# Spectral filter and SoLU expert on one core: a later landing of the transposes in the plan that orders the instructions

## The chip, the cores and the metric

The kernel runs on one core of a Trainium2 chip. The metric is the device time of one execution in microseconds, and the number compared is the median over runs.

## The reference

x is (8, 3136, 256). For each of the 8 batches the sequence goes through a real FFT, is multiplied with a complex 256 x 256 matrix, gets a bias, is soft-thresholded at 0.01, and goes back through the inverse FFT. The 25,088 rows that come out then go through a two-matrix layer:

```python
h = x @ w_in                                  # 256 -> 1024
sm = softmax(h);  solu = h * sm
ln = (solu - mean(solu)) / sqrt(var(solu) + 1e-6) * g_ln
out = ln @ w_out                              # 1024 -> 256
```

## The kernel before

**The FFT.** 3136 is split as 98 x 32. Each batch goes through four small products on TensorE (fwd1, fwd2, inv1, inv2, with the complex product, mix, in the middle), with two round trips through DRAM (tiles s1 and s2). Values are carried as pairs of fp16 numbers, a high and a low part. Results of inv2 are written into a ring (ring_hi, ring_lo).

**The layer.** It works on 196 tiles of 128 rows, 24 or 25 in a batch. A tile takes three steps. moe_head multiplies the ring with w_in into two PSUM banks (ph, 12 matmuls), VectorE finds the maximum (nm), ScalarE the exponential and VectorE the product (u). moe_turn splits u into lh (ScalarE) and ll (GpSimd) and issues two DMAs from the SP queue that transpose them: lh into th, ll into tl, 128 x 1024 fp16 each. moe_tail multiplies th with both parts of w_out (16 matmuls) and tl with one (8 matmuls) into a bank po; ScalarE scales po into o, and one to three DMAs on the SP queue store it. There are three buffers each for th and tl, two each for lh and ll, four for u, two for o; of the 8 PSUM banks at most 5 are ph and at most 2 po.

**The order.** No engine's order is written by hand. A class Plan collects all operations with a key (their wished place), gives each a length in ns (weigh, L304), plays them through on a model of the five engines (order, L351), and issues them sorted by the start times of that model (issue, L341). In every step of order, each engine looks at the operations whose inputs are ready; among those that can start within 50 ns of the earliest it takes the one with the smallest key. The engine with the earliest start goes first. After that an operation's end tells when its readers are ready (plus a delay by engine, 90 ns for a DMA) and when its buffers come free. The model's times are used for the order alone: on the chip each engine runs its instructions in that order and waits on semaphores for the real landings. All instructions stand under line L349 in the trace, that of the call, so tiles tell them apart.

**A DMA in the model.** weigh gives it a time on the SP queue (length) and a time on a shared bus (moved): 1600 and 1500 ns for a transpose, 430 ns and bytes/270 for the others. order then does:

```python
op.end = free[e] = at + op.length
...
if op.moved:
    bus = max(bus, op.end) + op.moved
    op.end = bus + 2000.0
```

So in the model a transpose that finds queue and bus free ends 1600 + 1500 + 2000 = 5100 ns after its start.

Of the kernel before, what the change touches and what calls it, by code (L numbers as in the profile page):

```python
# [242 lines left out]
class Plan:  # L243
# [60 lines left out]
    def weigh(self, op, name, args, kw, ins, outs):  # L304
        if name == "dma_start":
            v = next(v for v in (*outs, *ins) if not isinstance(v, DramView))
            size = (v.rows[1] - v.rows[0]) * v.cells.size * mybir.dt.size(v.dtype)
            cross = kw.get("transpose", False)
            op.length += 1600.0 if cross else 430.0
            op.moved += 1500.0 if cross else size / 270.0  # L310
        elif op.engine == "tensor":
            moving = ins[-1]
            n = moving.cells.size * (4 if moving.dtype == F32 else 1) * 0.42 + 1
            name = ins[0].tile.kw["name"]
            op.split = 2 if "gb" in name else 4 if name == "fa16_s" else 1
            op.length += n / op.split
        else:
            big = max((v.cells.size for v in (*ins, *outs)), default=1)
            scalars = sum(v.cells.size == 1 for v in ins)
            if big == 1:  # L320
                scalars -= 2 if name == "tensor_tensor" else 1
            each = self.ELEMENT[op.engine]
            wide = [v for v in ins if v.cells.size > 1]
            sbuf = not any(v.tile.kind.banks for v in (*ins, *outs))
            if op.engine == "scalar" and sbuf:
                each = 0.87
            if op.engine == "gpsimd" and len(wide) == 2 and all(v.dtype == F32 for v in (*wide, *outs)):
                each = 2.12
            if op.engine == "vector" and sbuf and name in ("tensor_scalar", "tensor_copy") and big > 1:
                each, op.port = 0.545, True  # L330
            if op.engine == "vector" and sbuf and len(wide) == 2:
                op.port = True
            if op.engine == "gpsimd":
                op.port = True
            op.length += self.CALL[op.engine] + big * each + max(scalars, 0) * self.SCALAR[op.engine]
            if "accum_out" in kw and op.engine == "scalar":
                op.length += 92.0
            if ALU.pow in kw.values() or ALU.pow in args:
                op.length += 420.0
# [11 lines left out]
    def order(self):  # L351
        ready = {e: [] for e in self.ENGINES}
        free = dict.fromkeys(self.ENGINES, 0.0)
        waits, bus, split, port = {}, 0.0, 1, 0.0
        for op in self.ops:
            waits[op] = len(op.needs)
            for o in op.needs:
                o.next.append(op)
            if not op.needs:
                op.at = 0.0  # L360
                ready[op.engine].append(op)
        left = {t: len(t.users) for op in self.ops for t in op.tiles}

        turn, turns = {}, {}
        for t, op in sorted(((t, min(t.users, key=lambda op: op.seq)) for t in left), key=lambda x: (x[1].key, x[1].seq)):
            if t.kind.banks is None:
                turn[t] = turns.get(t.kind, 0)
                turns[t.kind] = turn[t] + 1
        done = []

        def may_start(op):
            at = max(free[op.engine], op.at, port if op.port else 0.0)
            taken = {}
            for t in op.tiles:
                if t.owner is None:
                    k = t.kind
                    n = len(k.placed) + taken.get(k, 0)
                    taken[k] = taken.get(k, 0) + 1
                    if turn.get(t, n) != n:
                        return np.inf  # L380
                    n -= k.bufs
                    if n >= 0:
                        at = max(at, k.freed[n] if n < len(k.freed) else np.inf)
                    if k.banks is not None:
                        n, spare = taken.get(k.banks, 0), k.banks.free
                        taken[k.banks] = n + 1
                        at = max(at, spare[n][0] if n < len(spare) else np.inf)
            return at

        while len(done) < len(self.ops):  # L390
            best = None
            for e in self.ENGINES:
                can = [(may_start(op), op) for op in ready[e]]
                if not can:
                    continue
                first = min(at for at, _ in can)
                if first == np.inf:
                    continue
                _, _, at, op = min((op.key, op.seq, at, op) for at, op in can if at <= first + self.PATIENCE)
                if best is None or at < best[0]:  # L400
                    best = at, op
            assert best is not None, "the plan is stuck"
            at, op = best
            e = op.engine
            ready[e].remove(op)
            if e == "tensor":
                if op.split != split:
                    at += 100.0 if split == 1 else 220.0
                split = op.split
            op.start = at  # L410
            op.end = free[e] = at + op.length
            if op.port:
                port = op.end
            if op.moved:
                bus = max(bus, op.end) + op.moved
                op.end = bus + 2000.0
            for t in op.tiles:
                if t.owner is None:
                    t.owner = op
                    t.kind.placed.append(t)  # L420
                    if t.kind.banks is not None:
                        t.bank = t.kind.banks.free.pop(0)[1]
                left[t] -= 1
                if not left[t]:
                    freed = max(o.end + self.SEEN[o.engine] for o in t.users)
                    insort(t.kind.freed, freed)
                    if t.kind.banks is not None:
                        insort(t.kind.banks.free, (freed, t.bank))
            for o in op.next:
                waits[o] -= 1  # L430
                if not waits[o]:
                    o.at = max(p.end + (0.0 if p.engine == o.engine == "tensor" else self.SEEN[p.engine]) for p in o.needs)
                    ready[o.engine].append(o)
            done.append(op)
        self.span = max(op.end for op in done)
        return sorted(done, key=lambda op: (op.start, op.seq))
# [830 lines left out]
```

## Time and profile before

| | |
|---|---|
| median of 3 runs | 1628.03 us (1625.98 to 1630.09) |
| the profiled execution | 1626.85 us |
| its span, first to last instruction | 1625.1 us |
| TensorE (PE) matmuls busy | 1564.6 us (96%) |
| VectorE (DVE) busy | 1332.9 us (82%) |
| ScalarE (ACT) busy | 1242.8 us (76%) |
| GpSimd (POOL) busy | 1121.0 us (69%) |
| mean granted TensorE clock | 0.985 |

PE stands for matmuls and PEld for the weight loads that run beside them; the weights of the product with w_out are th and tl, so a late transpose shows first as a wait of PEld and then of PE. SPq is the SP queue, which issues every DMA. A matmul's end is modelled from its own latency, so matmuls that follow each other closely overlap in the records.

### The profile page before, as it was taken

The page shows a single profiled execution, that of the slowest core. Times are in us where ns is not written, and L with a number is a line of the kernel's source. Part 1 is how long each engine was busy: PE and PEld are TensorE (multiplying, and loading weights), DVE is VectorE, ACT ScalarE, POOL GpSimd, SP SyncE. Part 2 cuts the span into 40 slices and gives each one's busy share as a digit, 9 for nine tenths or more (in the row PEclk, how much of TensorE's full clock was granted, in tenths as well). Part 3 has the DMA queues.
Part 4 walks back from the last instruction along what each step waited for, and adds up shares of the span by engine and source line. Part 5 has one row for each costly group of instructions (what it writes and reads, how often), then busy time and mean ns, then how long its engine had stood idle before and what let it go on. Part 6 is the DMA issues. An engine that isn't in the chain of part 4 may idle for free.

```text
span 1625.1 us, 39102 instructions
## 1 busy us (share of the span) xinstructions
PE 1564.6 (96%) x13328; PEld 1107.1 (68%) x13328; DVE 1332.9 (82%) x3423; ACT 1242.8 (76%) x2576; POOL 1121.0 (69%) x1890
## 2 busy tenths in 40 slices
PE   5979999899999999999999999999999999999998
PEld 3645877468765777667766687666776577776675
DVE  4779899988998888887978789788887879877774
ACT  4667777886788867897778877788678877788886
POOL 0555777657875688667876578766876677776775
PEclk8989999999999999999999999999999999999999
DMA  8878987898898975789669995789857994587765
GB/s 235 272 226 209 230 230 173 205 221 216 200 210 169 209 175 127 161 185 213 161 126 171 190 200 132 147 177 205 188 124 148 181 198 124 128 156 146 141 130 110
DMA packets 540649, 290.30 MB, mean 179 GB/s; under 512 B 429660, under 2 KB 505982, under 8 KB 540450
## 3 DMA queue, kind: packets, MB, share of 16 engines
q1 hardware_dynamic: 540450, 287.81, 78.8%
q8 instruction: 104, 1.70, 0.4%
q14 instruction: 95, 0.78, 0.1%
HBM read 107.88 MB, written 77.07 MB: 114 GB/s over the span
## 4 chain that ended last, share of the span: by engine, by line
PE 79%; DMA 7%; DVE 5%; ACT 4%; issue 2%; POOL 1%; SPq 1%; DVEq 0%; ACTq 0%; POOLq 0%
PE po L349 27%; PE ph L349 24%; PE pf L349 23%; PE pb L349 4%; DMA th<-lh 3%; DMA tl<-ll 2%; DVE u L349 1%; ACT u L349 1%; SPq L349 1%; DVE nm L349 1%; POOL ll L349 1%; ACT junk L349 1%; DVE xl L349 1%; ACT lh L349 0%; DMA zt<-s2f 0%
## 5 line engine op out<-in xcount | busy, mean ns | idle before, releaser
L349 POOL TENSOR_TENSOR ll<-u,lh 128x1024 f16<-128x1024 f32 x196 | 420.6, 2146 | 136.5 <-ACT lh L349 111.1
L349 PE MATMUL po<-wout,th 128*128 128x256 f16 x3136 | 379.7, 275 | 18.2 <-DMA th<-lh 18.0
L349 PEld LDWEIGHTS <-th 128*128 128x128 f16 x3136 | 305.1, 99 | 88.7 <-DMA th<-lh 26.3
L349 ACT ACTIVATE u<-ph,m,hsb 128x512 f32<-128x512 f32 x384 | 296.1, 777 | 75.0 <-DVE m L349 74.7
L349 DVE TENSOR_REDUCE nm<-ph 128x1 f32<-128x512 f32 x392 | 265.8, 686 | 91.9 <-PE ph L349 90.5
L349 DVE SCALAR_TENSOR_TENSOR u<-ph,ch,u 128x512 f32<-128x512 f32 x392 | 282.2, 748 | 28.5 <-ACT u L349 12.7
L349 PE MATMUL ph<-win_hi,ring_hi 128*128 128x512 f16 x768 | 291.9, 380 | 1.2 <-DVE u L349 1.2
L349 PE MATMUL ph<-win_low,ring_lo 128*128 128x512 f16 x768 | 291.5, 380 | 0.0
L349 PE MATMUL ph<-win_lo,ring_hi 128*128 128x512 f16 x768 | 291.5, 380 | 0.0
L349 ACT CAST lh<-u 128x1024 f16<-128x1024 f32 x196 | 205.4, 1048 | 78.3 <-DVE u L349 74.4
L349 PEld LDWEIGHTS <-ring_hi 128*128 128x128 f16 x1536 | 145.7, 98 | 137.8 <-issue 10.8
L349 ACT ACTIVATE junk<-u,total 128x1024 bf16<-128x1024 f32 x196 | 226.0, 1153 | 6.4 <-POOL total L349 6.3
L349 PE MATMUL po<-wout,tl 128*128 128x256 f16 x1568 | 203.9, 273 | 9.1 <-DMA tl<-ll 9.1
L349 POOL TENSOR_TENSOR y<-yt,yc 128x512 f32<-128x512 f32 (+1 forms) x104 | 136.6, 1314 | 69.8 <-ACT yt L349 33.1
L349 PEld LDWEIGHTS <-tl 128*128 128x128 f16 x1568 | 150.6, 98 | 42.8 <-DMA tl<-ll 12.7
L349 PE MATMUL pf<-w_hi,Xl 128*128 128x256 f16 (+1 forms) x546 | 148.8, 273 | 1.1 <-DVE Xl L349 1.1
L349 PE MATMUL pf<-w_hi,Xh 128*128 128x256 f16 (+1 forms) x546 | 149.2, 273 | 0.0
L349 PE MATMUL pf<-w_lo,Xh 128*128 128x256 f16 (+1 forms) x546 | 148.8, 273 | 0.0
L349 POOL TENSOR_TENSOR yl<-y,yh 128x512 f16<-128x512 f32 (+1 forms) x104 | 124.0, 1193 | 34.0 <-ACT yh L349 32.3
L349 PEld LDWEIGHTS <-ring_lo 128*128 128x128 f16 x768 | 75.2, 98 | 91.0 <-DVE peaks L349 0.3
L349 ACT ACTIVATE o<-po,r 128x256 f32<-128x256 f32 x196 | 93.4, 476 | 56.2 <-PE po L349 42.6
L349 PEld LDWEIGHTS <-Xh 128*128 128x128 f16 (+1 forms) x1196 | 113.5, 99 | 26.4 <-issue 1.9
(197 smaller groups left out, 2843.1 us busy)
## 6 DMA issues: line engine op xcount, KB each, us to landing
xt<-in_x_dram SPq DMA_DIRECT2D x60, 392.0 KB
zt<-s SPq DMA_DIRECT2D x56, 392.0 KB
s<-zout SPq DMA_DIRECT2D x42, 512.0 KB
xt<-in_x_dram SPq DMA_DIRECT2D x96, 192.0 KB
s<-av SPq DMA_DIRECT2D x96, 192.0 KB
bin<-s SPq DMA_DIRECT2D x36, 512.0 KB
out_dram<-o SPq DMA_DIRECT2D x128, 96.0 KB
out_dram<-o SPq DMA_DIRECT2D x136, 64.0 KB
```

What stands on the lines that cost most here:

```text
L349: getattr(engine, name)(*args, **kw)
```

## The change

A transpose gets a further attribute, late, of 3000 ns (0 for any other DMA), and order adds it to the time at which the model believes that it has ended. The time on the SP queue and on the bus stay as they were. No operation, buffer, size or key changes.

```diff
             cross = kw.get("transpose", False)
             op.length += 1600.0 if cross else 430.0
             op.moved += 1500.0 if cross else size / 270.0
+            op.late = 3000.0 if cross else 0.0
...
             if op.moved:
                 bus = max(bus, op.end) + op.moved
-                op.end = bus + 2000.0
+                op.end = bus + 2000.0 + op.late
```

## Rows read from the trace of the kernel before

**Rows 1.** The page, part 1: busy time, share of the span and instructions of each engine.

```profile
PE 1564.6 (96%) x13328; PEld 1107.1 (68%) x13328; DVE 1332.9 (82%) x3423; ACT 1242.8 (76%) x2576; POOL 1121.0 (69%) x1890
```

**Rows 2.** The page, part 4: the chain that ended last, shares of the span by engine.

```profile
PE 79%; DMA 7%; DVE 5%; ACT 4%; issue 2%; POOL 1%; SPq 1%; DVEq 0%; ACTq 0%; POOLq 0%
```

**Rows 3.** Waits, whole span: who waited for whom, us in total, times, longest us.

```profile
PEld L349 <- DMA th<-lh: 26.3, 23, 4.7
...
PE po L349 <- DMA th<-lh: 18.0, 14, 4.6
...
POOL ll L349 <- DMA tl<-ll: 20.5, 11, 3.9
...
PEld L349 <- DMA tl<-ll: 12.7, 11, 1.8
...
PE po L349 <- DMA tl<-ll: 9.1, 10, 1.5
```

**Rows 4.** Groups of instructions: busy us, mean ns of one, idle before and its releasers.

```profile
L349 POOL TENSOR_TENSOR ll<-u,lh 128x1024 f16<-128x1024 f32 x196 | 420.6, 2146 | 136.5 <-ACT lh L349 111.1 <-DMA tl<-ll 20.5 <-ACT u L349 2.9
...
L349 PE MATMUL ph<-win_hi,ring_hi 128*128 128x512 f16 x768 | 291.9, 380 | 1.2 <-DVE u L349 1.2
```

**Rows 5.** Windows of 50 us: busy time (instructions) by engine, granted clock, DMA share, GB/s.

```profile
50.00:100.00 50.00, 50.00 (x347) 27.39 (x347) 36.76 (x64) 36.32 (x73) 35.47 (x30) 1.00 0.78 247
...
300.00:350.00 50.00, 42.46 (x361) 28.04 (x359) 41.97 (x128) 40.58 (x82) 28.17 (x57) 0.93 0.94 209
...
600.00:650.00 50.00, 50.00 (x472) 36.53 (x472) 41.96 (x109) 37.61 (x84) 42.55 (x64) 1.00 0.57 126
...
1250.00:1300.00 50.00, 46.23 (x366) 29.26 (x365) 44.05 (x117) 44.14 (x88) 30.95 (x64) 0.99 0.90 181
```

**Rows 6.** Timeline around the longest stall: start us, us, engine, work, idle before and releaser.

```profile
315.58 0.57 SPq L349 DMA_DIRECT2D zt<-s  x1
...
321.47 3.60 PE L349 MATMUL po<-wout,th 128*128 128x256 f16 x16 [4.59 <-DMA th<-lh]
...
324.86 2.03 PE L349 MATMUL pf<-ia_s,zt 98*128 98x98 f16 x24
...
328.00 0.39 PE L349 MATMUL ph<-win_hi,ring_hi 128*128 128x512 f16 x1
```

**Rows 7.** Timeline of two more stalls, and of the SP queue ahead of the second.

```profile
913.76 3.53 PE L349 MATMUL po<-wout,th 128*128 128x256 f16 x16 [2.32 <-DMA th<-lh]
...
1289.55 3.88 SPq L349 DMA_DIRECT2D xt<-in_x_dram  x7
...
1294.80 1.28 SPq L349 DMA_TRANSPOSE th<-lh  x1
...
1298.11 2.40 PE L349 MATMUL po<-wout,th 128*128 128x256 f16 x16 [2.59 <-DMA th<-lh]
```

**Rows 8.** Windows around the drops of the clock, and the last stage.

```profile
320.90:331.00 10.10, 9.53 (x64) 6.62 (x65) 4.52 (x20) 5.18 (x12) 4.16 (x7) 0.72 0.87 200
...
913.00:924.90 11.90, 11.14 (x85) 7.33 (x86) 9.62 (x33) 9.45 (x20) 8.09 (x16) 0.86 1.06 207
...
1299.40:1302.80 3.40, 3.40 (x30) 1.36 (x28) 3.01 (x12) 3.40 (x7) 2.18 (x4) 0.50 1.20 136
1425.00:1608.00 183.00, 183.00 (x1431) 127.10 (x1429) 136.45 (x404) 149.76 (x305) 128.98 (x264) 1.00 0.74 139
```

**Rows 9.** The chain in order of time: start us, us, what (a DMA: issue to release).

```profile
1124.77 7.06 DMA tl<-ll
...
1613.27 3.08 DMA th<-lh
```

**Rows 10.** Timeline of the last two waits of PE.

```profile
1613.57 1.05 PE L349 MATMUL po<-wout,tl 128*128 128x256 f16 x8 [0.41 <-DMA tl<-ll]
1616.39 3.21 PE L349 MATMUL po<-wout,th 128*128 128x256 f16 x16 [1.78 <-DMA th<-lh]
```

**Rows 11.** Groups of the stretch 1420 to 1610, columns as in rows 4.

```profile
L349 PE MATMUL po<-wout,th 128*128 128x256 f16 x557 | 66.5, 273 | 0.0
```

## The prediction

> **What bounds the kernel now.** I read the totals first. PE's matmuls are busy for 96% of the span, and no other engine for more than 82% [rows 1]; the chain that ended last runs over PE for 79% and over DMAs for 7% [rows 2]. So PE sets the pace, and what can be won is the time in which PE stands or runs slowly. The waits say where it stands: 18.0 us for th and 9.1 us for tl, 27.1 us in 24 waits [rows 3], of some 60 us that PE idles in all (1625.1 - 1564.6 [rows 1]). Waits of PE for anything computed are nearly absent: the first matmul of ph, the group behind which VectorE's delay would show, lost 1.2 us in 768 [rows 4]. The plan's picture of the engines is thus good, and what it misjudges are these two transposes.
>
> The windows show when. In stretches like 600 to 650 us PE has no gap, at a DMA share of 0.57; in 300:350 and 1250:1300 it lacks 7.5 and 3.8 us, at shares of 0.94 and 0.90 [rows 5]. The timeline shows what a stall costs beyond its gap. The longest took 4.59 us, and the 16 matmuls behind it 3.60 us [rows 6]; the granted clock of 320.9:331 is 0.72, between the levels of 2.4 and 1.2 GHz, and after a stall of 2.59 us [rows 7] it is 0.50, all of it at 1.2 GHz [rows 8]. In the last stage, with the layer alone, PE is busy for 183.0 of 183.0 us at full clock [rows 8].
>
> Two things make a th late. It may land late: 7.06 us from issue to release in a crowded stretch, against 3.08 us for the last tile, when little else is under way [rows 9]. Or it is issued late: before the 2.59 us stall the SP queue spent 3.88 us on seven loads of xt, and only then, behind a store, issued a transpose, at 1294.80 [rows 7].
>
> **The change, part by part.** *The belief.* A transpose in the model ends 1.6 + 1.5 + 3.0 + 2.0 = 8.1 us after its start on a free queue, instead of 5.1. The chip needs 3.08 to 7.06 us [rows 9]: 5.1 covers the quiet case and not the crowded one, 8.1 covers both. Queue and bus time stay the same, so other DMAs end where they did in the model. No instruction is added: 392 transposes, 4704 matmuls on po and the stores remain, only their places change.
>
> *PE.* The 16 + 8 matmuls of a tile's po come up to 3 us later in the order, behind the next ph, inv2 or fft product that is ready. Removed are the waits, but not those at the very end, 0.41 and 1.78 us [rows 10], where nothing is left to put in front: 27.1 - 2.2 = 24.9 us. What is put in front must exist. The longest waits have no such supply: 4.59, 2.32 and 2.59 us [rows 6, 7], together 9.5. At the longest the next work on PE was inv2, whose zt was issued at 315.58, and the next ph waited for what inv2 writes [rows 6]; with a landing of 3.1 us or more from issue, only about half of that stall could be filled. I take half of these three and the other 15.4 us in full: 4.7 + 15.4 = 20.1 us.
>
> *The clock.* Drops cost 10.1 x 0.28 + 11.9 x 0.14 + 3.4 x 0.50 = 2.8 + 1.7 + 1.7 = 6.2 us [rows 8]; each follows one of the long waits, and I count them as gone once these are halved.
>
> *ACT, SP and VectorE.* The scaling into o and its stores (392 DMAs) move back by the same time, past transposes and loads on the SP queue. A store that waits for o in that queue holds up the transposes behind it, but the plan now puts it where a later po will have finished, so I cost this at nothing; the cover is the two o buffers and the slack between a landing of 3.08 and the planned 8.1 us. If that cover is gone, a transpose slips by what the store lacks and PE meets it as today.
>
> *Buffers.* The model holds lh and ll until the transpose ends. For ll that is 2.15 us of GpSimd [rows 4] + 0.16 + 8.1 + 0.09 = 10.5 us, over two buffers 5.25 us a tile; PE takes 5.46 us a tile in the last stage, inv2's share with it (557 / 16 = 34.8 tiles in 190 us [rows 11]). So in the model's dense stretches the ll loop draws nearly level with PE. On the chip it ends earlier, and GpSimd's wait for a transpose of tl to give an ll free, 20.5 us in 11 waits [rows 3], stays off the path. Unpriced by any row is what the new spacing costs PE. Its bounds: below nothing, a gain of some 2.6 us if the last ph comes ahead of one more tile's po; above, the whole of today's waits, 27.1 us. I take 2.3 us, near the small waits for computed data of today [rows 4].
>
> *Sum.* 20.1 + 6.2 - 2.3 = 24.0 us off 1625.1 gives a span of 1601.1. The profiled execution took 1.75 us beyond its span, and the median lies 1.2 us above that execution: 1604.05, say 1604 us. At best all waits go, read on the weight loads (26.3 + 12.7 = 39.0 [rows 3]) with the clock's 6.2: 1583 us.
>
> The Trainium skill (Perfetto Trace Analysis, Identifying the Most-Contended Engine) warns that matmul busy time flatters PE, since pipelined matmuls look otherwise in a trace, and points to the weight loads. Here the two do differ, 27.1 against 39.0 us of waits; by the weight loads the sum would be about 1592 us, with the 11.9 us more taken in full. I keep the matmul rows, because a weight load that waits while earlier matmuls still stream costs nothing.
>
> **The rivals.**
>
> *A: the waits only move* (no change, 1624 to 1632 us). Stalls stand where loads, lh and ll are late together; GpSimd waits for tl there too [rows 3]. If the supply of tiles itself is late, PE stands a little further on, for ph or inv2. For it: the SP queue's 3.88 us of loads ahead of a transpose [rows 7], which no belief about landing shortens. Against it: PE has fft products of later batches, and no gap in uncrowded stretches [rows 5]. A form of it: the transposes never were late on landing, and 5.1 us was already too much. Then the 3 us shuffle the order for nothing: also about 1628 us. What decides is whether landings beyond 5.1 us are frequent; the 7.06 us of [rows 9] speaks against it.
>
> The Trainium skill (Advanced Engine Details and Errata, X-Bar Transpose (TRN2)) has transposing DMAs as fast as regular ones; that would favour this form. The trace disagrees: the last stage, mostly transposes and stores, moved 139 GB/s at a DMA share of 0.74, plain loads at 50:100 247 GB/s at 0.78 [rows 5, 8].
>
> *B: the ll loop paces the layer* (slower). The model believes 8.1 us everywhere, also in the dense stretches, where the chip needs 3.08. With 10.5 us a pair of buffers, and a transpose that finds another in the SP queue up to 1.6 us later, its loop is (10.5 + 1.6) / 2 = 6.05 us a tile against PE's 5.46 [rows 11]. The order would then space ph by the slower loop and put po ahead of ph that could run, and PE would meet waits where it has none. If half of the 0.59 us a tile comes through on the 35 tiles of the last stage, that is 10 us with today's waits kept: 1638 us; all of it, 21 us, gives 1649. For it: PE's 183.0 of 183.0 us can only get worse. Against it: an order spaced too widely is still run as fast as the data allow. It decides from the point at which the last stage's period is above 5.5 us a tile.
>
> *C: the order hardly changes,* since the smallest key among what is ready decides: within 2 us of 1628. Against it: ready times enter directly, and 3 us is sixty times the 50 ns of tolerance.
>
> **How the numbers follow.** The forecast has 0.60, A with its form 0.15, B 0.21, C 0.04. The likeliest case alone spans 1588 to 1620. Taking in A and C and the nearer price of B, the range is 1588 to 1639. A measurement of this kernel tells about 0.3%, or 5 us, from no change. Some of A's chance lies a little below that bound and is counted as faster: 0.62 faster, 0.16 same, 0.22 slower.
>
> **What would show it.** Right: the waits of PE for th and tl fall from 27.1 to under 12 us, no stretch of the middle has a granted clock under 0.95, the gap from a transpose's issue to its po grows by 1 to 3 us, the last stage still has PE without a gap. Wrong by A: the sum of PE's waits stays near 27 us under other names (ph for u, inv2 for zt, or th again). Wrong by B: in 1425:1608 PE's busy time is below its window, with waits for u, ph or th. The prediction as a whole fails if the busy time of PE itself grows, or if the fft stages before the first tile, which hold no transpose, get longer.

## The result, and the profile after

The change made the kernel slower by 0.4%, little but clear of noise: 1633.92 us median (1630.36 to 1635.5, 13 runs) against 1625.98 us before (1622.88 to 1630.55, 13 runs), a ratio of 1.0044 with a 95% interval of 1.0033 to 1.0056. Forecast was 1604 us.

The profiled execution took 1632.97 us, with a span of 1631.2 us. The page's busy times, and the shares of its chain by engine, answer to [rows 1] and [rows 2]:

```profile
PE 1564.5 (96%) x13328; PEld 1107.3 (68%) x13328; DVE 1327.9 (81%) x3423; ACT 1234.3 (76%) x2576; POOL 1120.7 (69%) x1890
...
PE 70%; ACT 8%; DMA 7%; DVE 6%; issue 3%; POOL 3%; SPq 2%; ACTq 0%; DVEq 0%; POOLq 0%
```

PE has the same work as before, 1564.5 us, and stands for 1631.2 - 1564.5 = 66.7 us where it stood for 60.5. That difference of 6.2 us is the whole of the longer span (6.1 us), so nothing but PE's gaps has to be explained. Of the 6.2 us, 1.4 lie ahead of the first po, which starts at 149.76 us and not at 148.29; two later kernels with the same two orders (g1 and g2 below) have it at 149.99 and 147.87, so single executions differ by as much there. The mean granted clock is 0.985 in both. The waits of PE after the first tile of the layer answer to [rows 3] (in total, times, longest):

```profile
PE pf L350 <- DMA bin<-s: 11.0, 5, 3.7
...
PE ph L350 <- DVE u L350: 5.0, 5, 2.3
PE pf L350 <- DMA zt<-s: 3.8, 2, 2.4
PE pf L350 <- DVE Xl L350: 3.3, 5, 1.0
PE po L350 <- DVE u L350: 3.2, 3, 1.2
PE po L350 <- DMA tl<-ll: 2.7, 2, 1.6
...
PE po L350 <- DMA th<-lh: 0.2, 1, 0.2
```

The waits that the change was to remove are gone: 27.1 us for th and tl before, 2.9 us now. In their place PE waits 11.0 us for bin, the input of fwd2, and 3.8 us for zt, the input of inv2, for neither of which it had waited so before. As much again is for other engines: after the first tile PE's waits for VectorE and ScalarE rise from 2.6 to 16.8 us, 14.6 of them within the stretches around the batch boundaries that the next section names. The windows, in answer to [rows 5] and [rows 8], show that the places are the same (length, then busy time of PE, PEld, DVE, ACT and POOL with instructions, granted clock, DMA share, GB/s):

```profile
300.00:350.00 50.00, 42.70 (x365) 27.32 (x358) 42.40 (x119) 40.53 (x79) 26.64 (x50) 1.00 0.87 202
1250.00:1300.00 50.00, 47.45 (x391) 31.21 (x389) 40.54 (x106) 42.62 (x86) 29.75 (x57) 0.97 0.90 184
1425.00:1608.00 183.00, 183.00 (x1422) 126.10 (x1421) 135.05 (x412) 145.65 (x309) 128.71 (x270) 1.00 0.71 140
```

In 300:350 PE lacks 7.3 us (7.5 before), in 1250:1300 2.6 us (3.8), and in the last stage nothing, as before. How one wait turned into another stands in the timelines, here at the batch boundary near 750 us. Before, from the issue of the batch's first loads of bin to the fwd2 that needs them:

```profile
736.48 1.29 SPq L349 DMA_DIRECT2D bin<-s  x2
...
736.80 1.91 PE L349 MATMUL po<-wout,th 128*128 128x256 f16 x16
...
740.21 1.05 PE L349 MATMUL po<-wout,tl 128*128 128x256 f16 x8 [1.50 <-DMA tl<-ll]
...
742.38 0.83 PE L349 MATMUL pf<-fb,bin 128*128 128x128 f16 x12
```

and after:

```profile
747.74 1.24 SPq L350 DMA_TRANSPOSE th<-lh  x1
...
750.40 1.17 SPq L350 DMA_DIRECT2D bin<-s  x2
...
755.24 0.84 PE L350 MATMUL pf<-fb,bin 128*128 128x128 f16 x12 [1.93 <-DMA bin<-s]
...
755.92 1.91 PE L350 MATMUL po<-wout,th 128*128 128x256 f16 x16
```

Before, PE had a whole tile's po to do while bin was under way, 24 matmuls, and fwd2 came 5.9 us after the issue, without a wait of its own (po had waited 1.50 us for a tl). After, no po stands there: PE has 12 matmuls of ph and the end of an inv2, stands for 1.93 us until bin lands, and starts fwd2 at 755.24, 4.8 us after the issue. Directly behind fwd2 it takes a th whose transpose (counted through, the n-th transpose to the n-th po) was issued at 747.74, 8.2 us earlier, sooner than the load of bin. Transposes in this kernel were released some 3 to 7 us after their issue [rows 9], so this one had most likely landed; the plan believed that it would not be there until 8.1 us after its issue. The other boundaries are alike. Before, at least 24 matmuls on po started between the issue of a batch's first bin and its first fwd2, at each of the six boundaries with such a load, and PE never waited there. After, at the five where PE waits, there are 0 to 22, and fwd2 comes 4.2 to 4.8 us after the issue, where it had come after 4.6 to 6.1.

### The profile page after: what moved, and what is told of

The parts are those of the page before. It is cut to its first block, busy times and chain, and to the rows that moved or that the text cites. A ratio compares the mean times of both kernels' runs of the same rounds, so it can differ in the third digit from the quotient of the medians.

```text
span 1631.2 us, 38958 instructions
## 1 busy us (share of the span) xinstructions
PE 1564.5 (96%) x13328; PEld 1107.3 (68%) x13328; DVE 1327.9 (81%) x3423; ACT 1234.3 (76%) x2576; POOL 1120.7 (69%) x1890
## 4 chain that ended last, share of the span: by engine, by line
PE 70%; ACT 8%; DMA 7%; DVE 6%; issue 3%; POOL 3%; SPq 2%; ACTq 0%; DVEq 0%; POOLq 0%
PE po L350 23%; PE pf L350 21%; PE ph L350 21%; PE pb L350 4%; DMA xt<-in_x_dram 3%; SPq L350 2%; ACT u L350 2%; ACT junk L350 2%; DVE u L350 2%; POOL ll L350 1%; DMA bin<-s 1%; ACT lh L350 1%; DVE nm L350 1%; POOL r L350 1%; ACT xh L350 1%
## 5 line engine op out<-in xcount | busy, mean ns | idle before, releaser
L350 PE MATMUL po<-wout,th 128*128 128x256 f16 x3136 | 375.5, 273 | 5.4 <-DVE u L350 3.2
```

The lines of the kernel that those rows point to most:

```text
L350: getattr(engine, name)(*args, **kw)
```

## The experiments

Each was measured against the kernel before on the same chip; the ratio and its 95% interval are to that. PE's loss is counted as its gaps after the first tile of the layer, plus half of each stretch there at 1.2 GHz that comes before the last 25 us. For the kernel before that is 30.2 + 6.8 = 37 us. It lies nearly all in the six stretches around the batch boundaries (290 to 400, 495 to 605, 690 to 800, 880 to 995, 1070 to 1190, 1255 to 1400 us) and in the last 25 us.

**Which half of the change: readers or buffers, and how much.** Four kernels, each one edit on the changed kernel. e1 tells only the readers of the later landing, e2 only the freeing of buffers (late is 0.0 for every other operation):

```diff
 e1
-                op.end = bus + 2000.0 + op.late
+                op.end = bus + 2000.0
-                    o.at = max(p.end + (0.0 if ...
+                    o.at = max(p.end + p.late + (0.0 if ...
 e2
-                op.end = bus + 2000.0 + op.late
+                op.end = bus + 2000.0
-                    freed = max(o.end + self.SEEN[o.engine] ...
+                    freed = max(o.end + o.late + self.SEEN[o.engine] ...
 e3
-            op.late = 3000.0 if cross else 0.0
+            op.late = 1000.0 if cross else 0.0
 e4
+            op.late = 2000.0 if cross else 0.0
```

e1: 

> Only the readers of a transpose are told of the later landing; the buffers lh, ll, th and tl come free in the model as before the change. Theory 1 (the later place of po is itself what costs: po no longer stands ahead of the first fwd2 of a batch, and PE waits there for bin): as the changed kernel, PE waits for th and tl under 5 us, for bin about 11 us, time 1631 to 1636 us. Theory 2 (the model's longer hold of lh and ll spaces the layer): the waits for th and tl are gone and nothing takes their place, 1600 to 1615 us. Theory 3 (any other order is some 0.5% off by chance): anything from 1618 to 1640 us, with waits that fit neither.

e2: 

> Only the freeing of the buffers is 3 us later in the model; the readers are told the old landing. Theory 1: PE waits for th and tl stay near 27 us, none for bin, time as before, 1622 to 1630 us. Theory 2: the loss of the change is here, with today's waits kept: 1632 to 1645 us. Theory 3: 1618 to 1640 us.

e3: 

> The change with 1 us in place of 3. Theory 1: the waits for th and tl fall to about half (14 us), those for bin stay under 4 us, time 1615 to 1625 us, faster than both. Theory 2: a third of the loss, 1628 to 1630 us. Theory 3: no trend with the size, 1618 to 1640 us.

e4: 

> The change with 2 us in place of 3. Theory 1: waits for th and tl under 8 us, for bin 4 to 9 us, time 1620 to 1631 us, between the size of 1 us and that of 3. Theory 2: two thirds of the loss, 1630 to 1632 us. Theory 3: no trend, 1618 to 1640 us.

The last column is PE's waits after the first tile for anything but a DMA: VectorE, ScalarE and GpSimd.

| kernel | median us | ratio | PE waits for th + tl | for bin | for other engines |
|---|---|---|---|---|---|
| before | 1625.98 beside the change, 1627.99 beside e1 to e4 | 1 | 27.1 us | 0 us | 2.6 us |
| the change, 3 us | 1633.92 | 1.0044 (1.0033 to 1.0056) | 2.9 us | 11.0 us | 16.8 us |
| e1, readers only | 1631.26 | 1.0021 (1.0009 to 1.0033) | 2.4 us | 4.0 us | 18.6 us |
| e2, buffers only | 1641.9 | 1.0086 (1.0070 to 1.0103) | 18.2 us | 2.5 us | 15.2 us |
| e3, 1 us | 1640.5 | 1.0079 (1.0062 to 1.0096) | 17.6 us | 4.1 us | 13.4 us |
| e4, 2 us | 1646.04 | 1.0109 (1.0092 to 1.0126) | 7.0 us | 9.4 us | 21.4 us |

With 1, 2 and 3 us the waits follow theory 1: told a later landing, the plan trades waits for th for waits for bin, step by step. e1, which by theory 1 should wait 11 us for bin, waits 4.0 (its traced execution, 1626.48 us, is the fastest of its twelve). The times follow no theory: 1 us costs more than 3, 2 us most, and the buffers alone cost four times as much as the readers. No sum of the two halves gives the whole. Theory 2 had the time of e2, but wanted e1 at 1600 to 1615 us, e3 and e4 below 1632. All five are slower than before, without an order that any of the prediction's terms could give, and in all five PE waits 13 to 21 us for other engines, which no theory had named. That left theory 3, that the order before is simply a good one among many, though e2, e3 and e4 lie above the 1640 us that it had as its bound.

**Changes that mean nothing, and two that mean something.** e5 makes the landing 0.1 us later; e6 has the kernel before with another constant, of VectorE, moved by 5 ns. e7 is the change with 5 us. e8 attacks the new wait itself: the loads of bin are believed 4 us later too.

```diff
 e5
+            op.late = 100.0 if cross else 0.0
 e6
-    SEEN = dict(tensor=250.0, vector=160.0, scalar=190.0, ...
+    SEEN = dict(tensor=250.0, vector=165.0, scalar=190.0, ...
 e7
+            op.late = 5000.0 if cross else 0.0
 e8
+            op.late = 3000.0 if cross else 4000.0 if any(o.tile.kw["name"] == "bin"
+                for o in outs if not isinstance(o, DramView)) else 0.0
```

e5: 

> The change with 0.1 us in place of 3: too little to mean anything for where a transpose lands. Theory S (the order is reshuffled by any change, an order's time scatters over some 20 us, and the order before sits at the low end of that): 1630 to 1646 us, with PE's waits after the first tile at 33 us or more. Theory 1 (the later place of po is what costs): an order nearly as before, 1623 to 1631 us, th and tl still waited for by 20 us or more.

e6: 

> The kernel before, with one unrelated constant of the plan moved by 5 ns (a result of VectorE is seen 165 ns after its end, not 160). Theory S: 1630 to 1646 us, like the runs with 1 and 2 us. Theory 1: as before, 1623 to 1631 us.

e7: 

> The change with 5 us in place of 3. Theory S: no trend, 1630 to 1646 us. Theory 1: the waits for bin and what stands behind po grow past those at 3 us (11 us for bin), 1638 to 1655 us; PE's waits for th and tl are nil.

e8: 

> The change, and the loads of bin believed 4 us later as well, so that the first fwd2 of a batch is placed later. Theory 1: PE's 11 us of waits for bin go, and the time falls to 1618 to 1626 us. Theory S: the waits for bin go, but as many come elsewhere, 1630 to 1646 us.

Measured: e5 1635.3 us, 1.0060 (1.0040 to 1.0079); e6 1644.99 us, 1.0104 (1.0088 to 1.0120); e7 1645.47 us, 1.0106 (1.0084 to 1.0128); e8 1638.61 us, 1.0077 (1.0059 to 1.0096). A meaningless 5 ns costs more than the change. The time of e7 lies in the range of theory 1 too, but its waits do not fit it: 8.8 us for th and tl, which were to be nil, and 9.8 for bin, which were to pass 11. The waits of PE in e6:

```profile
PE po L349 <- DMA th<-lh: 14.4, 16, 3.3
...
PE po L349 <- DMA tl<-ll: 11.9, 14, 2.0
...
PE pf L349 <- DMA zt<-s: 5.2, 1, 5.2
```

and in e8, where those for bin were to go:

```profile
PE pf L350 <- DMA zt<-s: 8.5, 4, 3.3
...
PE po L350 <- DMA tl<-ll: 4.5, 6, 1.7
...
PE pf L350 <- DMA bin<-s: 0.4, 1, 0.4
```

In e6 PE waits 26.3 us for th and tl, about as before, and 5.2 for one zt on top. In e8 the waits for bin went from 11.0 to 0.4 us, as meant, and those for zt rose from 3.8 to 8.5. The waits for other engines stay at 19.1 us there (16.8 with the change). So another order gives the waits other names, transfers and engines alike. This is theory S as to the scatter: nine orders by now, all between 1631 and 1646 us, the one before below them all. It says nothing yet on why there is something to wait for.

**What the boundaries lack: first the SP queue.** The SP queue issues DMAs for 0.8 to 0.9 of the time in most of each boundary (worked out as the share of 20 us slices that its DMA issues cover in the trace; mostly 0.3 to 0.6 in between). So theory Q was that issues are short there. f1 joins the 48 + 1 rows of each half in fwd1 into one DMA; f2 and f3 issue the stores of s1 from ScalarE's queue, f3 with the change; f4 does so with the stores of the output.

```diff
 f1
-        return slice(half * P // 2, half * P // 2 + F1 - 1), slice(half * P // 2 + F1 - 1, half * P // 2 + F1)
+        return (slice(half * P // 2, half * P // 2 + F1),)
 f2, and f3 on the changed kernel
-                    nc.sync.dma_start(to[rows.start ...
+                    nc.scalar.dma_start(to[rows.start ...
 f4
-            nc.sync.dma_start(out_v[b, n2, n1 : n1 + n], o[p : p + n])
+            nc.scalar.dma_start(out_v[b, n2, n1 : n1 + n], o[p : p + n])
```

f1: 

> The kernel before, with the 49 rows of each half in fwd1 loaded and stored by one DMA, not by one of 48 rows and one of a single row: 192 fewer issues on the SP queue (about 0.35 us each, all at the batch boundaries). Theory Q (the SP queue, which issues for 0.9 of the time at each boundary, sets the stalls there; the order of PE only gives them another name): SP's share at the boundaries falls to about 0.8, PE's loss (gaps and half clock after the first tile, 37 us before) falls by a third or more, 1600 to 1618 us. Theory D (the DMA engines' full share there sets them): no gain, 1625 us or more, since 49 rows spread less evenly over 16 engines. Theory S alone (any order scatters, no common cause): 1630 to 1646 us, loss 37 us or more.

f2: 

> The kernel before, with the 192 stores of s1 issued from ScalarE's queue; bytes and transfers stay the same. Theory Q: SP's share at the boundaries falls under 0.8, PE's loss by a third or more, 1600 to 1618 us, unless ScalarE's waits for av eat it. Theory D: the stalls stay, 1625 us or more. Theory S alone: 1630 to 1646 us.

f3: 

> The changed kernel (3 us later landing) with the same move of the stores of s1 to ScalarE's queue. Theory Q: also 1600 to 1618 us, and now at or below the same move without the change, since what is left of the stalls is late landing. Theory 1 (the later place of po costs): slower than the same move without the change by 6 us or more. Theories D and S: 1630 to 1646 us.

f4: 

> The kernel before, with the stores of the output (392, less the few of the tiles that span two batches) issued from ScalarE's queue. Theory Q: SP's share falls by about a tenth everywhere, PE's loss at the boundaries by a quarter or more, 1605 to 1622 us. Theories D and S: 1630 to 1646 us.

Measured: f1 1682.91 us, 1.0367 (1.0350 to 1.0384); f2 1708.64 us, 1.0522 (1.0507 to 1.0537); f3 1675.55 us, 1.0314 (1.0296 to 1.0332); f4 1640.3 us, 1.0101 (1.0083 to 1.0118). All four miss what theory Q expected. In f2 the move itself did harm, by ScalarE's own waits:

```profile
ACT o L349 <- DMA s<-av: 67.2, 11, 7.8
```

Ahead of its scaling into o ScalarE stood for 67.2 us behind stores that it now issues, and ahead of all its work for 115 us in 19 such waits, so f2 and f3 tell nothing of the SP queue; that f3 is the faster by 33 us is one pair of orders more. f4 is the cleaner trial: SP's share of those slices fell to between 0.6 and 0.85 for the most part, yet PE's loss at the second to sixth boundary is 20 us, against 23 before, and in the first it rose from 11 to 21. In f1 a single store of s1 became longer to issue. The issues of that tile (min/median/max ns, first and last start), of the kernel before:

```profile
L349 SPq DMA_DIRECT2D s<-av x192: 221/309/1294, 291.3 to 1309.5; - x192
```

and of f1:

```profile
L349 SPq DMA_DIRECT2D s<-av x96: 269/428/1735, 289.3 to 1358.0; - x96
```

Half as many issues take nearly as long in sum, 62.5 us against 67.0. The loads of xt did become cheaper to issue, 72.8 us in sum against 132.2, but the issues of the transposes grew from 550 to 622 us and those of the output's stores from 202 to 225. In all SP issued for 1109 us where it had been 1074, so f1 did not relieve the queue. PE's waits for th and tl in f1:

```profile
PE po L349 <- DMA th<-lh: 46.4, 25, 4.5
...
PE po L349 <- DMA tl<-ll: 14.0, 16, 2.6
```

That is 60.4 us, not 27.1. The issues were fewer and these stalls doubled, with the same bytes in transfers of 49 rows. Why is open: no run tests the reason that theory D gave.

**What the boundaries lack: then the bytes.** g1 and g2 leave the order alone. On every engine their instructions stand in the same sequence as in the kernel before and in the changed one, because the plan is told the old size; only the loads of x bring less, from the fourth batch on, so that neither computes the right output. 290.3 MB become 270.2 MB.

```diff
+        q = n // 4 if b > 2 else n
+        nc.believed = n // q
-        nc.sync.dma_start(t, x[b]...[c])
+        nc.sync.dma_start(t[:, :q], x[b]...[c][:, :q])
+        nc.believed = 1
...
+                    gs_n = 1 if b > 2 else 2
+                    nc.believed = 2 // gs_n
-                    nc.sync.dma_start(xt[rows].rearrange("p (g m) -> p g m", g=2), xv[c, r][n1])
+                    nc.sync.dma_start(xt[rows].rearrange("p (g m) -> p g m", g=2)[:, :gs_n], xv[c, r][n1][:, :gs_n])
+                    nc.believed = 1
...
-            op.moved += 1500.0 if cross else size / 270.0
+            op.moved += 1500.0 if cross else size * self.believed / 270.0
```

g1: 

> The order of before, every instruction in its place, but from the fourth batch's front on the two kinds of loads of x bring fewer bytes: a quarter of the columns for the peaks, half for fwd1 (the rest of the tile keeps older data; the plan is told the old size). Theory D (the DMA engines, full at each batch boundary, make transposes and loads late there, whatever stands in which place): PE's loss at the boundaries from the second on falls from 23 us to under 12, the first boundary, whose bytes are unchanged, keeps its 11 us; 1608 to 1618 us. Theory Q (the number of issues on the SP queue, which is unchanged): 1622 to 1630 us.

g2: 

> The order of the changed kernel with the same smaller loads of x. Theory D: also 12 us or so below its own full loads, 1616 to 1625 us, and the difference to the order of before shrinks. Theory 1 (the later place of po costs by itself): 8 us or more above the order of before with the same loads. Theory Q: 1630 to 1636 us.

Measured: g1 1609.08 us, 0.9887 (0.9867 to 0.9907); g2 1611.05 us, 0.9903 (0.9885 to 0.9920), faster than the 1616 to 1625 us of theory D. The windows at the six boundaries, first of the kernel before (length, busy time of PE, PEld, DVE, ACT, POOL with instructions, granted clock, DMA share, GB/s):

```profile
290.00:400.00 110.00, 102.46 (x942) 74.19 (x941) 94.30 (x248) 85.79 (x175) 71.98 (x121) 0.97 0.95 219
495.00:605.00 110.00, 105.11 (x959) 75.80 (x957) 92.88 (x243) 83.65 (x173) 75.00 (x124) 1.00 0.85 188
690.00:800.00 110.00, 107.38 (x1014) 79.27 (x1012) 91.95 (x229) 87.81 (x181) 81.01 (x129) 1.00 0.86 187
880.00:995.00 115.00, 111.82 (x1045) 82.54 (x1043) 95.22 (x238) 88.62 (x183) 79.60 (x134) 0.99 0.86 184
1070.00:1190.00 120.00, 116.13 (x1113) 85.97 (x1113) 100.93 (x246) 96.80 (x202) 88.21 (x147) 1.00 0.85 185
1255.00:1400.00 145.00, 140.08 (x1275) 100.88 (x1274) 121.27 (x299) 112.88 (x236) 103.92 (x172) 0.99 0.77 165
```

and of g1:

```profile
290.00:400.00 110.00, 104.04 (x954) 75.11 (x954) 95.61 (x250) 86.95 (x178) 73.77 (x123) 0.97 0.87 199
495.00:605.00 110.00, 106.65 (x982) 77.78 (x981) 94.14 (x249) 85.33 (x177) 78.09 (x129) 1.00 0.79 179
690.00:800.00 110.00, 109.03 (x1029) 80.63 (x1026) 93.07 (x235) 89.55 (x190) 83.23 (x134) 1.00 0.84 177
880.00:995.00 115.00, 113.77 (x1086) 84.90 (x1083) 96.70 (x239) 91.12 (x192) 82.49 (x134) 1.00 0.77 175
1070.00:1190.00 120.00, 118.96 (x1110) 87.88 (x1108) 102.52 (x247) 96.68 (x202) 90.47 (x146) 1.00 0.75 170
1255.00:1400.00 145.00, 142.90 (x1351) 105.63 (x1350) 122.52 (x297) 110.64 (x235) 103.64 (x170) 1.00 0.72 159
```

Taking PE's busy time from the length: before, PE lacks 7.5, 4.9, 2.6, 3.2, 3.9 and 4.9 us; in g1 6.0, 3.4, 1.0, 1.2, 1.0 and 2.1 us. From the second boundary on that is 19.5 us against 8.7, and the clock there has no more drops (two of 1.7 us before). The first boundary, with most of its bytes unchanged, keeps most of its loss. The DMA share of the six stretches goes from 0.77 to 0.95 down to 0.72 to 0.87. So theory D holds: with the same instructions in the same order, and as many issues, PE's stalls halve when the DMA engines have less to move. The same in the changed order: from the changed kernel to g2 PE's waits after the first tile go from 34.6 to 18.9 us, those for DMAs from 17.7 to 7.2 and those for other engines from 16.8 to 11.8. The queue is not wholly out of it, since a smaller load is also quicker to issue: SP issues for 1037 us in g1, not 1074, and over the six stretches its share is 0.75 to 0.61 (0.78 to 0.68 before). But f4 took it down nearly as far there, 0.76 to 0.59, and from the second boundary on PE's loss was still 20 us, if in another order.

The packets in the trace of the kernel before tell what fills the DMA engines. Those of 256 bytes, 1024 to a transpose by their number, are 102.8 of 290.3 MB but take 10.0 of 20.6 ms of packet time: 10.2 bytes per ns, against 18.7 for those of 1024 bytes. So the transposes themselves are half of that load.

PE's waits for th and tl in g1:

```profile
PE po L350 <- DMA th<-lh: 8.6, 5, 3.1
...
PE po L350 <- DMA tl<-ll: 4.4, 6, 1.4
```

13.0 us, against 27.1 before, for transposes that nothing was done to.

The Trainium skill (Perfetto Trace Analysis, What "DMA-bound" means) names, among the places to look at, the DMA engines themselves and the issuing engine's sequencer, the latter when its track is solid with DMA slices. SP's track at 0.8 to 0.9 looks like the second; g1, where the issues are as many and the stalls halve, puts this kernel with the first.

With the smaller loads the two orders are at 0.9903 (changed) and 0.9887, intervals that overlap. This fits the reading that where there is less to wait for, it matters less which wait the order meets.

**Has the change an effect of its own?** Two more pairs of orders, with VectorE's constant at 165 and 155 ns, with and without the change; and one kernel before with a slower bus in the plan.

```diff
 g3: the change with vector=165.0;  g4: before with vector=155.0;  g5: the change with vector=155.0
 g6
-            op.moved += 1500.0 if cross else size / 270.0
+            op.moved += 1700.0 if cross else size / 220.0
```

g3: 

> The change, on top of the unrelated 5 ns for VectorE's results (1645 us without the change). Theory L (the later landing is worth something, but the order before is a lucky one that any change loses): 8 us or more below 1645, 1625 to 1637 us. Theory S alone: anything from 1630 to 1646 us, without a tie to the run without the change. Theory 1: above 1645 us.

g4: 

> The kernel before with VectorE's results seen 155 ns after their end, not 160, no change to the landing. Theories S and L: 1630 to 1646 us. If it stays at 1628 us or below, the order before is not at the low end of the scatter.

g5: 

> The change on top of VectorE's results seen at 155 ns (1634.7 us without the change). Theory S (the change has no effect of its own, it draws another order): 1628 to 1646 us, and over the three pairs with and without the change (160, 165, 155 ns) no common sign. Theory L (the later landing is worth something): 1627 us or less. Theory 1 (the later place of po costs): 1641 us or more.

g6: 

> The kernel before, with the plan's DMA bus as slow as the full stretches show (220 bytes per ns in place of 270, 1.7 us of bus for a transpose in place of 1.5), no later landing. Theory D+ (the plan's bus is too fast, so it lets PE run ahead of full DMA engines at the boundaries; told of it, it spreads the loads): 1612 to 1624 us, faster than both kernels. Theory S: 1628 to 1646 us, since the bytes at the boundaries stay.

| VectorE's constant | without the change | with it |
|---|---|---|
| 160 ns | 1 | 1.0044 (1.0033 to 1.0056) |
| 165 ns | 1.0104 (1.0088 to 1.0120) | 1.0112 (1.0091 to 1.0132) |
| 155 ns | 1.0052 (1.0035 to 1.0068) | 1.0095 (1.0078 to 1.0112) |

In two pairs the change costs 0.4%, in the third it makes no difference, in none does it gain. Theory L falls. Whether the change costs a little by itself, as theory 1 says (which had put g3 above 1645 and g5 at 1641 us or more, and got 1646.41 and 1643.19), or three draws fell this way, three pairs do not settle; another order by itself moves the time by 0.5 to 1.0%. g6 came out at 1643.91 us, 1.0105 (1.0090 to 1.0120): telling the plan of slower DMA engines did not help either; its bytes are the same. No kernel that computes the whole beat the one before; e1 came nearest, at 1.0021.

## Why the prediction was wrong

**What bounds the kernel: half right.** PE sets the pace, and its gaps account for the whole difference between the kernels. Wrong was the end of its first paragraph, that what the plan misjudges are "these two transposes". It took the name of a wait for its cause. The windows of [rows 5] had what g1 points to beside it: DMA shares of 0.94 and 0.90 where PE stalls, 0.57 where it does not. th was the transfer that this order met first.

**The belief: right, and of no use.** As far as PE's waits tell, 8.1 us does cover the landings: those for th and tl fell to 2.9 us, below the 12 us that I had named as the sign of success. The time from a transpose's issue to its po grew as meant, from 5.9 to 9.1 us in the median.

**PE: the step that failed.** "What is put in front must exist", it says, and it takes 20.1 of 24.9 us as filled. The work to put in front did exist; what the term left out is what po had been standing in front of. po had itself been cover for the load of bin, and with it gone PE waits at five of the six boundaries, 11.0 us. The longest stall, 4.59 us for th, became one of 2.45 us for zt, ahead of the inv2 behind it. Waits for bin and zt make 14.8 us, and those for VectorE and ScalarE rose by 14.2 us, together 29.0. The waits for th and tl did fall by 24.2 us, more than the 20.1 of the term, but as a gain nothing of it arrived. At a boundary PE has little to spare, because the fft work there waits for transfers through the same DMA engines, which g1 and g2 show to be short. For the waits for other engines this holds only in part (16.8 us with the change, still 11.8 in g2); what else makes them in the changed order is open.

**The clock: mis-sized.** 6.2 us were counted as gone; the mean granted clock stayed at 0.985. Half of the time at 1.2 GHz in the six stretches is 6.8 us before and 6.8 us after: the drops moved with the stalls (1250:1300 is at 0.97 now, 550:600 at 0.93, under the 0.95 that was named).

**The new spacing: mis-sized.** 2.3 us were taken, near the small waits for computed data of before, with 27.1 us, "the whole of today's waits", as the upper bound. The waits for computed data alone rose by the 14.2 us above. Net of everything the change lost 6.1 us of span, so the new waits come to about 27.1 - 2.9 + 6.1 = 30 us, beyond even that bound. I bounded it by today's waits as if an order could not be worse than this one; every other order tried that computes the whole was.

**ACT, SP and VectorE: right.** The scaling into o and its stores were not in the way: SP's waits for o fell from 124.3 to 84.7 us.

**Buffers: right.** The last stage still has PE at 183.0 of 183.0 us, so the ll loop does not pace the layer and rival B is out as its mechanism, though the time moved its way. Buffers alone (e2) cost 1641.9 us, but that kernel too has no gap in the last stage, and its loss lies at the boundaries.

**The rivals.** Rival A named what happened, down to its signs: "ph for u, inv2 for zt", and a supply that is late. It was given 0.15 and a time of 1624 to 1632 us, as if moved waits had to sum to the same; after the first tile they went from 29.7 to 34.6 us. Against it I had set that PE has fft products of later batches; at the boundaries these wait as well. The row on seven loads of xt ahead of a transpose [rows 7] was A's best witness and was read as a detail.

**The range** held the measured 1633.92 us, since it took in A and the nearer price of B, and the chance of slower stood at 0.22. What was wrong is the likeliest case and its sign; that the time lies within is no merit of the mechanism.

## What to carry to other kernels

Where waits cluster in a few stretches and a shared resource is nearly full in the same stretches, moving the waiting instruction may only change the name of the wait, as here; less of what fills the resource shortened it (20 MB of 290 gave 1.1%). Before a wait's removal is counted as a gain, ask what the moved work was covering. And when an order comes out of a planner, measure two or three orders that differ by nothing (a constant moved by 5 ns): here that scatter, 0.5 to 1.0%, is larger than the change.

## What was not expected of the hardware

A DMA of 49 rows instead of 48 + 1 was no saving on the issuing queue as a whole: the loads of xt took 59 us less to issue, but the median issue of a store of s1 went from 309 to 428 ns, the transposes' issues took 72 us more, and the kernel lost 3.7%. Issuing the 192 stores of s1 from ScalarE's queue made that engine stand for 67.2 us ahead of its scaling into o, in 11 waits of up to 7.8 us, and for 115 us ahead of all its work, by the profile's account of who ended each wait. And a transpose's packets of 256 bytes moved 10.2 bytes per ns on a DMA engine, packets of 1024 bytes 18.7.
